# Attention and SiLU-GLU on one core: weights split into two fp32r parts at conversion, stored and reloaded as a pair

## The chip, the cores and the metric

The kernel runs on one core of a Trainium2 chip. Its engines are TensorE (PE: matmuls, with weight loads listed apart as PEld), VectorE (DVE), ScalarE (ACT), GpSimd (POOL) and SyncE (SP, which here issues every DMA). Each works through its own queue in order, and semaphores order them against each other. The metric is the time of one execution on the device in microseconds, as the median of several runs.

## The reference

Two stages, the second on the result of the first. q, k and v are float32 of shape (8, 8, 576, 64), omega is (128, 64). The three MLP weights are float64.

```python
def phi(x):                       # random features, m = 128
    proj = einsum('bhsd,md->bhsm', x, omega)
    h = proj - sum(x * x, -1) / 2
    return exp(h - max(h, -1)) / sqrt(m)
q_p, k_p = phi(q * scale), phi(k * scale)
kv = einsum('bhsm,bhsd->bhmd', k_p, v);  z = sum(k_p, axis=2)
attn = (q_p @ kv) / (q_p @ z + 1e-6)

x = attn as (4608, 512)           # tokens x model
g, val = x @ w_gate, x @ w_val    # 512 x 1536 each
out = ((g * sigmoid(g)) * val) @ w_out   # 1536 x 512
```

## The kernel before

**Attention** runs in 72 steps. Each takes two groups of 256 rows of one pair of heads: loads them (`nat`), transposes them on PE (`pt`, `st_transpose`), projects them (`pp`), takes sums of squares (`sq` on POOL) and maxima (DVE) and the exponentials (`ph` on ACT). Groups of k then add to `kvacc`. Groups of q give, through further transposes and products, columns of x, which are kept on chip as a high and a low fp32r part: ACT copies the high part (`xh`, L626) and DVE subtracts for the low part (`xl`, L627). From the step `DENSE` on, the transposes, `po` and `xt` share one PSUM bank (`ps_att`).

**The MLP** treats x as ten tiles of 512 columns (the first and last of 256), in four rounds of two or three tiles. Its hidden dimension is cut into 12 pieces f of 128, in four sets of three. A visit is one tile with one set: three gate products (`g`), the down products (`o`) of the visit before, three value products (`v`), with SiLU, the product and the split of the hidden values (`hh` on ACT, `hl` on POOL) between. Every product is made of three fp32r matmuls: high with high, and high with low both ways. Only one set of weights is on chip. Within a round the sets change three times, so that over four rounds there are 12 switches of nine weight pieces each: 108 reloads. Rounds go through the sets in alternating direction, so none is needed between rounds.

**The weights.** [...] `convert_all` turns 36 pieces of 128 x 512 float64 values into float32 (`u`) with integer and float operations on the two 32-bit halves: an absolute value on ACT (L260), five operations on DVE (L262 to L270), an add on POOL (L272). It is a generator: each `tick()` emits its next part, at a pace set by `marks`, and `need(f, i)` runs it on until piece (f, i) has been marked as converted. A raw piece is 512 KB and lies in one of two buffers (`stw`); its load is written one piece ahead. Each `u` is stored in DRAM (`wscr`, L275). The nine pieces of the first set are also split at once by `split_piece`: ACT casts to fp32r (`whi`, L242), POOL subtracts (`wlo`, L243). All others are reloaded by `load_weights` (L294) into a float32 buffer (`wraw`, three buffers, shared with `u`) and split there, as soon as PE has made its last use of the weights that they replace.

**What sets the order.** The program text is emitted step by step, with `give` mixing the MLP's work into the attention steps. Tile, the framework, then puts the instructions of each engine's queue in its own order, by when it expects them to be ready, hands out the buffers of a tag, and adds all semaphores. So a queue's order isn't that of the text: in the trace, POOL squares the input of step 66 at 811.7 us, while PE transposes it at 867.9 us.

Of the kernel before, what the change touches and what calls it, by code (L numbers as in the profile page):

```python
# [11 lines left out]
F32 = mybir.dt.float32  # L12
F32R = mybir.dt.float32r
I32 = mybir.dt.int32
U32 = mybir.dt.uint32
AF = mybir.ActivationFunctionType
ALU = mybir.AluOpType
# [6 lines left out]
def kernel(  # L24
# [11 lines left out]
    nc = tc.nc  # L36
    B, H, S, D = q.shape
    M = omega.shape[0]
    NT, DM = out.shape
    DF = w_gate.shape[1]  # L40
    P = 128
# [4 lines left out]
    NF = DF // P  # L46
# [3 lines left out]
    FA = 3  # L50
# [27 lines left out]
    wpool = ctx.enter_context(tc.tile_pool(name="wpool", bufs=FA))  # L78
    moe = ctx.enter_context(tc.tile_pool(name="moe", bufs=2))
    accp = ctx.enter_context(tc.tile_pool(name="accp", bufs=10))  # L80
    dram = ctx.enter_context(tc.tile_pool(name="dram", bufs=1, space=DRAM))
    ps_m = ctx.enter_context(tc.tile_pool(name="ps_m", bufs=4, space=PSUM))
    att = ctx.enter_context(tc.tile_pool(name="att", bufs=2))
# [36 lines left out]
    def slots(n, kind):  # L120

        if not 0 <= n < NS:
            return []
        return [(i, b, g, (kgroups if kd == "k" else qgroups)[g]) for i, (kd, b, g) in enumerate(steps[n]) if kd == kind]
# [87 lines left out]
    E_LO = float(np.uint32(896 << 20).view(np.float32))  # L212
    E_HI = float(np.uint32(1151 << 20).view(np.float32))

    wscr = dram.tile([NF, 3, P, DM], F32, name="wscr")
    raws = {}

    def load_raw(n):
        if n < 3 * NF:
            f, i = divmod(n, 3) if n >= 3 * FA else (n % FA, n // FA)  # L220
            w = (wg32, wv32, wo32)[i]
            raw = att.tile([P, 2 * DM], I32, name=f"st{f}_{i}", tag="stw")
            raws[n] = f, i, raw
            if i < 2:
                nc.sync.dma_start(
                    raw.rearrange("p (c f) -> p c f", f=2 * P),
                    w[:, f * 2 * P : (f + 1) * 2 * P].rearrange("(c p) f -> p c f", p=P),
                )
            else:
                nc.sync.dma_start(raw, w[f * P : (f + 1) * P, :])  # L230

    weights = {}
    converted = set()

    def new_weights(f, i):
        hi = wpool.tile([P, DM], F32R, name=f"whi{f}_{i}", tag=f"whi{i}")
        lo = wpool.tile([P, DM], F32R, name=f"wlo{f}_{i}", tag=f"wlo{i}")
        weights[f, i] = hi, lo

    def split_piece(f, i, raw):  # L240
        hi, lo = weights[f, i]
        nc.scalar.copy(hi, raw)  # L242
        nc.gpsimd.tensor_tensor(lo, raw, hi.bitcast(F32), op=ALU.subtract)  # L243

    OPS = 7

    def convert_all():


        load_raw(0)  # L250
        for n in range(3 * NF):
            load_raw(n + 1)
            f, i, raw = raws.pop(n)
            if f < FA:
                new_weights(f, i)
            u = moe.tile([P, DM], F32, name=f"wc{f}_{i}", tag="wraw", bufs=3)
            pairs = raw.rearrange("p (n t) -> p n t", t=2)
            low, r = pairs[:, :, 0], pairs[:, :, 1].bitcast(F32)
            ri, ui = r.bitcast(I32), u.bitcast(I32)
            nc.scalar.activation(u, r, AF.Abs)  # L260
            yield
            nc.vector.tensor_scalar(u, u, E_LO, E_HI, op0=ALU.max, op1=ALU.min)  # L262
            yield
            nc.vector.tensor_scalar(ui, ui, 3, 0x3FFFFFFF, op0=ALU.logical_shift_left, op1=ALU.bitwise_and)
            yield
            nc.vector.scalar_tensor_tensor(ri, ri, -0x40000000, ui, op0=ALU.bitwise_and, op1=ALU.bitwise_or)
            yield
            nc.vector.tensor_single_scalar(ui, ri, -0x800000, op=ALU.bitwise_and)
            yield
            nc.vector.scalar_tensor_tensor(u, low.bitcast(U32), 2.0**-52, u, op0=ALU.mult, op1=ALU.mult)  # L270
            yield
            nc.gpsimd.tensor_tensor(u, r, u, op=ALU.add)  # L272
            if f < FA:
                split_piece(f, i, u)
            nc.sync.dma_start(wscr[f, i], u)  # L275
            converted.add((f, i))
            yield

    wa = convert_all()
    ticks = [0]  # L280

# [4 lines left out]
    def need(f, i):  # L286
        while (f, i) not in converted:
            tick()

    def load_weights(f, i):  # L290
        need(f, i)
        new_weights(f, i)
        raw = moe.tile([P, DM], F32, name=f"wraw{f}_{i}", tag="wraw", bufs=3)
        nc.sync.dma_start(raw, wscr[f, i])  # L294
        split_piece(f, i, raw)

# [158 lines left out]
    def load_z(n):  # L457

        for _, b, g, gr in slots(n, "q"):
            if g == 0 and b >= BPOOL:  # L460
                assert len(converted) == 3 * NF, "the raw weights' buffers are still needed"
                zt = att.tile([P, 2, 4, M], F32, name=f"zt{b}", tag="stw")
                for a2 in range(2):
                    nc.sync.dma_start(
                        zt[:, a2], zds.pop((b, a2)).rearrange("(o h) m -> o h m", o=1).broadcast_to([P, 4, M])
                    )
                    zbc[b, a2] = zt[:, a2]
# [195 lines left out]
    def down(j, k_, ht, wts, next_set, tt):  # L663
        fs = sorted(ht)
        po = ps_moe(f"o{j}_{k_}_{tt}", [P, DM])
        for n, f in enumerate(fs):
            need(f, 2)
            mm2(po, ht[f], weights[f, 2] if wts is None else wts[f], tt, n == 0, n == FA - 1)
        if k_ == 0:
            acc[j, tt] = accp.tile([P, DM], F32, name=f"acc{j}_{tt}", tag="acc")  # L670
            nc.scalar.copy(acc[j, tt], po)
        else:
            a_ = acc[j, tt]
            nc.vector.tensor_tensor(a_, po, a_, op=ALU.add)  # L674
        if k_ == NSET - 1:
            a_ = acc.pop((j, tt))
            for o in range(0, P, RES):
                nc.sync.dma_start(rows_of(TILES[j][0] + tt * P + o), a_[o : o + RES, :])
        if next_set is not None and tt == TILES[j][1] // P - 1:
            for n in range(FA):  # L680
                load_weights(next_set * FA + n, 2)

    def stream():

        todo = []
        for vi, (j, s_, k_) in enumerate(visits):
# [22 lines left out]
            if new_set:  # L709
                for f in fs:  # L710
                    load_weights(nxt[1] * FA + f - fs[0], 0)
# [3 lines left out]
            for f in fs:  # L715
                need(f, 1)
                pv = ps_moe(f"v{vi}_{f}", [P, T])[:, 0:w]
                mm1(pv, weights[f, 1], xs)
                yield mm1_us(w)
                h = pg[f]  # L720
                nc.vector.tensor_tensor(h, pv, h, op=ALU.mult)  # L721
                hh = moe.tile([P, T], F32R, name=f"hh{vi}_{f}", tag="hh", bufs=FA)[:, 0:w]
                hl = moe.tile([P, T], F32R, name=f"hl{vi}_{f}", tag="hl", bufs=FA)[:, 0:w]
                nc.scalar.copy(hh, h)  # L724
                nc.gpsimd.tensor_tensor(hl, h, hh.bitcast(F32), op=ALU.subtract)  # L725
                ht[f] = hh, hl
                if new_set:
                    load_weights(nxt[1] * FA + f - fs[0], 1)
# [47 lines left out]
    for n in range(NN):  # L776
        load(n + LA)
        load_v(n + LAV)
        want = OPS * np.interp(clock[n + 1], [clock[m] for m, _ in marks], [x for _, x in marks])
        for i, what in enumerate(ORDER):  # L780
            left = len(ORDER) - i
            what(n)
            due = course[n + 1] - given[0] - debt[0]
            if due > 0:
                give(due / left)
            for _ in range(int(np.ceil((want - ticks[0]) / left))):
                tick()
        load_z(n)
# [32 lines left out]
```

## Time and profile before

| | |
|---|---|
| Median of 3 runs | 1264.08 us (1259.43 to 1271.75) |
| Profiled execution | 1261.98 us |
| Its span, first to last instruction | 1260.2 us |
| Mean granted clock of PE | 0.986 |
| Busy PE / PEld / DVE / ACT / POOL | 1222.5 / 1004.1 / 526.1 / 632.5 / 506.2 us |
| First raw load / last conversion add | 12.2 us / 356.3 us |
| First / last reload of a weight piece | 199.8 us / 1192.4 us |
| Last exponential of the attention | 982.6 us |

The profile is of one execution. A line names a source line (L243), an engine, an operation, and what is written and read (`wlo<-wraw,whi`); `x108` is a count. "Busy" is the time in which an engine executes; matmuls overlap in their pipeline, so their listed durations add up to more than the time they take. Waits name the engine whose signal came last. "PEclk" or the last but two of a stage's columns is the share of PE's full clock that was granted. Times to landing of a DMA run from issue to the last byte.

### The profile page before, as it was taken

How to read it: one execution, taken by the hardware profiler on the slowest of the kernel's cores; microseconds unless marked ns; L12 is line 12 of the kernel's file. 1: busy time of each engine (PE TensorE's matmuls, PEld its weight loads, DVE VectorE, ACT ScalarE, POOL GpSimd, SP SyncE). 2: the span in 40 equal slices, each digit the busy share in tenths (PEclk: the TensorE clock that was granted, in tenths of full speed). 3: DMA queues.
4: the chain of work that ended last, by engine and by line, in shares of the span. 5: the costliest groups of instructions: out<-in, count | busy, mean ns of one | idle time of the engine just before them, and what ended most of it. 6: DMA issues, size and time to landing. Idle time of an engine off the chain costs nothing.

```text
span 1260.2 us, 19027 instructions
## 1 busy us (share of the span) xinstructions
PE 1222.5 (97%) x7137; PEld 1004.1 (80%) x7137; DVE 526.1 (42%) x1080; ACT 632.5 (50%) x1368; POOL 506.2 (40%) x448
## 2 busy tenths in 40 slices
PE   6999999999899999999999999999999999999998
PEld 5888878888688878877777777877777778888887
DVE  4886795557732343334433433223343311121112
ACT  4887857564444645555556644853644323221211
POOL 3344444445442212644544334444654314242421
PEclk7999999999999999999999999999999999999999
DMA  6656555344521222222212221221211111010112
GB/s 161 152 139 154 141 146 172 106 137 122 159 67 52 61 65 60 76 67 62 65 51 67 68 59 38 64 65 45 52 50 30 39 25 50 25 51 25 51 30 55
DMA packets 157692, 97.80 MB, mean 78 GB/s; under 512 B 119680, under 2 KB 132000, under 8 KB 157600
## 3 DMA queue, kind: packets, MB, share of 16 engines
q1 hardware_dynamic: 157600, 96.59, 28.7%
q8 instruction: 56, 0.92, 0.3%
q14 instruction: 36, 0.29, 0.1%
HBM read 77.66 MB, written 18.89 MB: 77 GB/s over the span
## 4 chain that ended last, share of the span: by engine, by line
PE 67%; DVE 2%; POOL 2%; issue 1%; ACT 1%; DMA 0%; POOLq 0%; ACTq 0%
PE o L650 20%; PE g L641 19%; PE v L641 17%; PE pp L393 3%; PE kvacc L528 2%; PE ptq L552 2%; PE pt L370 2%; PE xt L607 1%; POOL jk L488 1%; PE po L569 1%; ACT ph L425 1%; DVE st L411 1%; DVE dj L492 0%; POOL wlo L243 0%; POOL hl L725 0%
## 5 line engine op out<-in xcount | busy, mean ns | idle before, releaser
L725 POOL TENSOR_TENSOR hl<-sl,hh 128x512 fp32r<-128x512 f32 (+1 forms) x120 | 145.3, 1211 | 223.0 <-ACT hh L724 222.9
L243 POOL TENSOR_TENSOR wlo<-wraw,whi 128x512 fp32r<-128x512 f32 x108 | 138.5, 1294 | 146.1 <-ACT whi L242 135.4
L425 ACT ACTIVATE ph<-pp,st 128x128 f32<-128x128 f32 x576 | 167.7, 387 | 57.7 <-DVE st L414 56.9
L641 PE MATMUL g<-xh,whi 128*128 128x512 f32 (+1 forms) x480 | 185.4, 387 | 0.0
L641 PE MATMUL v<-xh,whi 128*128 128x512 f32 (+1 forms) x480 | 184.3, 384 | 0.0
L641 PE MATMUL g<-xh,wlo 128*128 128x512 f32 (+1 forms) x480 | 179.8, 375 | 0.0
L641 PE MATMUL v<-xh,wlo 128*128 128x512 f32 (+1 forms) x480 | 179.3, 374 | 0.0
L641 PE MATMUL g<-xl,whi 128*128 128x512 f32 (+1 forms) x480 | 179.2, 373 | 0.0
L641 PE MATMUL v<-xl,whi 128*128 128x512 f32 (+1 forms) x480 | 178.5, 372 | 0.0
L650 PE MATMUL o<-whi,hh 128*128 128x512 f32 x432 | 176.5, 408 | 0.6 <-DVE sl L721 0.6
L650 PE MATMUL o<-whi,hl 128*128 128x512 f32 x432 | 169.9, 394 | 1.1 <-POOL hl L725 0.6
L650 PE MATMUL o<-wlo,hh 128*128 128x512 f32 x432 | 170.3, 394 | 0.0
L724 ACT CAST hh<-sl 128x512 fp32r<-128x512 f32 (+1 forms) x120 | 70.0, 583 | 174.5 <-DVE sl L721 174.1
L721 DVE TENSOR_TENSOR sl<-v,sl 128x512 f32<-128x512 f32 (+1 forms) x120 | 76.2, 635 | 172.2 <-PE v L641 167.9
L674 DVE TENSOR_TENSOR acc<-o,acc 128x512 f32<-128x512 f32 x108 | 74.1, 689 | 174.2 <-PE o L650 173.9
L377 POOL TENSOR_TENSOR sq<-nat 128x512 f32<-128x512 f32 x72 | 76.8, 1067 | 155.6 <-DMA nat<-in_k_dram 127.4
L411 DVE TENSOR_REDUCE st<-pp 128x4 f32<-128x512 f32 x144 | 93.5, 683 | 77.2 <-PE pp L393 77.1
L242 ACT CAST whi<-wraw 128x512 fp32r<-128x512 f32 x108 | 66.6, 622 | 97.3 <-PE v L641 55.3
L641 PEld LDWEIGHTS g<-xh,whi 128*128 128x128 f32 x480 | 91.6, 191 | 19.3 <-issue 4.2
L641 PEld LDWEIGHTS v<-xh,whi 128*128 128x128 f32 x480 | 91.0, 189 | 17.5 <-issue 2.7
L641 PEld LDWEIGHTS g<-xh,wlo 128*128 128x128 f32 x480 | 91.5, 191 | 15.9 <-issue 0.4
L641 PEld LDWEIGHTS v<-xh,wlo 128*128 128x128 f32 x480 | 91.0, 190 | 16.0 <-issue 0.5
(67 smaller groups left out, 1910.8 us busy)
## 6 DMA issues: line engine op xcount, KB each, us to landing
wraw<-wscr SPq DMA_DIRECT2D x108, 256.0 KB, 2.7
wscr<-wc SPq DMA_DIRECT2D x36, 256.0 KB, 2.3
out_dram<-acc SPq DMA_DIRECT2D x72, 128.0 KB, 2.3
nat<-in_k_dram SPq DMA_DIRECT2D x64, 128.0 KB, 3.2
v<-in_v_dram SPq DMA_DIRECT2D x64, 128.0 KB, 2.9
nat<-in_q_dram SPq DMA_DIRECT2D x64, 128.0 KB, 2.7
st<-in_moe_w_gate_dram SPq DMA_DIRECT2D x12, 512.0 KB, 4.2
st<-in_moe_w_val_dram SPq DMA_DIRECT2D x12, 512.0 KB, 4.6
```

Source lines behind the costliest of these rows:

```text
L242: nc.scalar.copy(hi, raw)
L243: nc.gpsimd.tensor_tensor(lo, raw, hi.bitcast(F32), op=ALU.subtract)
L377: nc.gpsimd.tensor_tensor(sq, nat, nat, op=ALU.mult)
L393: nc.tensor.matmul(pp[hh][:, i, c, :], x[r, i, c * P : (c + 1) * P], omT[r], start=True, stop=True)
L411: nc.vector.tensor_reduce(st[:, 1, :, :, hh], pp[hh], axis=AX.X, op=ALU.max, negate=True)
L425: nc.scalar.activation(ph[:, c, hh * M : (hh + 1) * M], pp[hh][:, i, c, :], AF.Exp, bias=st[:, 3, i, c, hh : hh + 1], scale=1.0,)
L641: nc.tensor.matmul(ps, a_[:, ws], b_[:, c, :], start=n == 0, stop=n == 3 * NC - 1)
L650: nc.tensor.matmul(ps, a_[:, ts_], b_, start=first and n == 0, stop=last and n == 2)
L674: nc.vector.tensor_tensor(a_, po, a_, op=ALU.add)
L721: nc.vector.tensor_tensor(h, pv, h, op=ALU.mult)
L724: nc.scalar.copy(hh, h)
L725: nc.gpsimd.tensor_tensor(hl, h, hh.bitcast(F32), op=ALU.subtract)
```

## The change

All 36 pieces are now split when they are converted. The nine pieces of the first set still go to their place on chip. For the other 27 the two parts, each 128 x 512 float32, are written over the raw float64 piece, which has just their size. High and low part are neighbours in one tile, so that each piece is stored by one DMA of 512 KB and reloaded by one DMA of 512 KB straight into the place from which PE reads; `split_piece` and the buffer `wraw` of the reloads are gone. A piece's store is written four DVE operations into the next piece (the last one's at the end), and only then does the piece count as converted. Raw buffers go from two to three (`zt`, which takes the same tag later, has three, too), and buffers for `u` from three to two.

```diff
-    wscr = dram.tile([NF, 3, P, DM], F32, name="wscr")
+    wscr = dram.tile([NF, 3, P, 2, DM], F32, name="wscr")
...
-            raw = att.tile([P, 2 * DM], I32, name=f"st{f}_{i}", tag="stw")
+            raw = att.tile([P, 2 * DM], I32, name=f"st{f}_{i}", tag="stw", bufs=3)
...
     def new_weights(f, i):
-        hi = wpool.tile([P, DM], F32R, name=f"whi{f}_{i}", tag=f"whi{i}")
-        lo = wpool.tile([P, DM], F32R, name=f"wlo{f}_{i}", tag=f"wlo{i}")
-        weights[f, i] = hi, lo
-
-    def split_piece(f, i, raw):
-        hi, lo = weights[f, i]
-        nc.scalar.copy(hi, raw)
-        nc.gpsimd.tensor_tensor(lo, raw, hi.bitcast(F32), op=ALU.subtract)
+        w = wpool.tile([P, 2, DM], F32R, name=f"w{f}_{i}", tag=f"w{i}")
+        weights[f, i] = w[:, 0], w[:, 1]
+        return w
...
+        def put_away(f, i, w):
+            nc.sync.dma_start(wscr[f, i], w.bitcast(F32))
+            converted.add((f, i))
+
         load_raw(0)
+        store = None
         for n in range(3 * NF):
             load_raw(n + 1)
             f, i, raw = raws.pop(n)
-            if f < FA:
-                new_weights(f, i)
-            u = moe.tile([P, DM], F32, name=f"wc{f}_{i}", tag="wraw", bufs=3)
+            u = moe.tile([P, DM], F32, name=f"wc{f}_{i}", tag="wraw", bufs=2)
...
             nc.vector.tensor_single_scalar(ui, ri, -0x800000, op=ALU.bitwise_and)
+
+            if store:
+                put_away(*store)
             yield
             nc.vector.scalar_tensor_tensor(u, low.bitcast(U32), 2.0**-52, u, op0=ALU.mult, op1=ALU.mult)
             yield
             nc.gpsimd.tensor_tensor(u, r, u, op=ALU.add)
-            if f < FA:
-                split_piece(f, i, u)
-            nc.sync.dma_start(wscr[f, i], u)
-            converted.add((f, i))
+
+            w = new_weights(f, i) if f < FA else raw.bitcast(F32R).rearrange("p (n f) -> p n f", n=2)
+            nc.scalar.copy(w[:, 0], u)
+            nc.gpsimd.tensor_tensor(w[:, 1], u, w[:, 0].bitcast(F32), op=ALU.subtract)
+            store = f, i, w
             yield
+        put_away(*store)
...
     def load_weights(f, i):
         need(f, i)
-        new_weights(f, i)
-        raw = moe.tile([P, DM], F32, name=f"wraw{f}_{i}", tag="wraw", bufs=3)
-        nc.sync.dma_start(raw, wscr[f, i])
-        split_piece(f, i, raw)
+        w = new_weights(f, i)
+        nc.sync.dma_start(w.bitcast(F32), wscr[f, i])
```

More of the change, by code (lines that the diff above doesn't have):

```diff
@@ L461, in load_z @@
                 assert len(converted) == 3 * NF, "the raw weights' buffers are still needed"
-                zt = att.tile([P, 2, 4, M], F32, name=f"zt{b}", tag="stw")
+                zt = att.tile([P, 2, 4, M], F32, name=f"zt{b}", tag="stw", bufs=3)
                 for a2 in range(2):
```

## The prediction, made before the change was run

> **What bounds the kernel now.** I read the page's busy times first, then the busy times by stage, and then what TensorE (PE) waited for.
>
> ```profile
> PE 1222.5 (97%) x7137; PEld 1004.1 (80%) x7137; DVE 526.1 (42%) x1080; ACT 632.5 (50%) x1368; POOL 506.2 (40%) x448
> ```
> ```profile
> 134.00:200.00 66.00, 62.53 (x413) 51.45 (x410) 53.99 (x116) 42.48 (x107) 26.82 (x22) 0.97 0.58 162
> 200.00:360.00 160.00, 153.40 (x853) 128.85 (x852) 95.56 (x164) 88.39 (x159) 77.64 (x62) 0.98 0.43 131
> ...
> 400.00:1050.00 650.00, 642.80 (x3593) 507.35 (x3590) 229.63 (x487) 341.00 (x703) 265.74 (x229) 1.00 0.21 54
> 1050.00:1261.00 211.00, 205.60 (x1038) 175.23 (x1036) 38.27 (x60) 51.03 (x94) 66.97 (x58) 1.00 0.16 43
> ```
> The columns are length, busy PE, PEld, DVE, ACT, POOL, clock, DMA share, GB/s. PE is the bound, and the change gives it the same matmuls. So only PE's idle time and its half clock can move: 650 - 642.80 = 7.2 us from 400 to 1050, 3.5 us from 134 to 200, 6.6 us from 200 to 360. In the conversion stage (134 to 200) DVE is busy for 53.99 of 66 us, so there a delay on DVE is nearest to PE.
>
> PE's waits, first from 400 to 1050, then from 0 to 400:
> ```profile
> PE pt L370 <- DVE xl L627: 5.7, 7, 2.0
> ```
> ```profile
> PE pt L370 <- DVE xl L627: 6.0, 1, 6.0
> ```
> One wait, seven times, makes 5.7 of the later 7.2 us: a transpose of new q and k needs the one PSUM bank that DVE's xl is still to read. What stood before xl is read from the timeline at the longest of the seven:
> ```profile
> 617.96 1.98 ACT L242 CAST whi<-wraw 128x512 fp32r<-128x512 f32 x3 [2.09 <-PE o L650]
> ...
> 620.23 3.77 POOL L243 TENSOR_TENSOR wlo<-wraw,whi 128x512 fp32r<-128x512 f32 x3
> ...
> 621.72 1.07 DVE L413 SCALAR_TENSOR_TENSOR st<-st 128x8 f32<-128x8 f32 x1
> 622.82 1.21 DVE L414 SCALAR_TENSOR_TENSOR st<-st 128x8 f32<-128x8 f32 x1
> ...
> 624.12 1.91 ACT L425 ACTIVATE ph<-pp,st 128x128 f32<-128x128 f32 x7 [4.19 <-DVE st L414]
> ...
> 627.25 0.41 DVE L627 TENSOR_TENSOR xl<-xt,xh 128x256 fp32r<-128x256 f32 x1
> ...
> 627.72 0.66 PE L370 MATMUL pt<-ident,nat 128*128 128x128 f32 x4 [2.00 <-DVE xl L627]
> ```
> ```profile
> L413 DVE SCALAR_TENSOR_TENSOR st<-st x72: 151/167/1209, 15.8 to 978.7; 128x8 f32<-128x8 f32 x72
> ```
> L413 has a median of 167 ns; it and L414 took 2.28 us together while POOL ran three weight splits: about 1.95 us too long (taking L413's median for both). The exponentials (L425) came later by that, and xl behind them. The next one:
> ```profile
> 821.24 3.78 POOL L243 TENSOR_TENSOR wlo<-wraw,whi 128x512 fp32r<-128x512 f32 x3 [8.51 <-ACT whi L242]
> ...
> 826.29 0.69 DVE L492 TENSOR_REDUCE dj<-jk 128x4 f32<-128x512 f32 x1 [4.96 <-POOL jk L488]
> ...
> 827.96 0.66 PE L370 MATMUL pt<-ident,nat 128*128 128x128 f32 x4 [1.20 <-DVE xl L627]
> ```
> Here jk stood behind three splits on POOL, and DVE, with xl queued, behind jk.
>
> **What is removed.** Each of 108 reloads loses one ACT cast and one POOL subtract:
> ```profile
> L243 POOL TENSOR_TENSOR wlo<-wraw,whi x108: 1268/1291/1492, 206.8 to 1203.6; 128x512 fp32r<-128x512 f32 x108
> ```
> ```profile
> L242 ACT CAST whi<-wraw x108: 605/621/643, 205.6 to 1201.7; 128x512 fp32r<-128x512 f32 x108
> ```
> By stage (length, then busy POOL in those instructions alone):
> ```profile
> 134.00:200.00 66.00, 1.34 (x1) 0.97 0.58 162
> 200.00:360.00 160.00, 27.45 (x21) 0.98 0.43 131
> 360.00:1261.00 901.00, 111.00 (x87) 1.00 0.20 52
> ```
> After 360 us POOL loses 111 us and ACT 87 x 0.621 = 54 us. PE gets only what waited for them, the two stalls above: 2.0 + 1.2 = 3.2 us. To that comes the clock:
> ```profile
> 625.00:630.00 5.00, 3.00 (x13) 2.16 (x12) 1.72 (x4) 2.67 (x9) 3.57 (x3) 0.83 0.24 67
> 630.00:635.00 5.00, 5.00 (x27) 4.28 (x25) 1.41 (x3) 0.81 (x2) 2.29 (x2) 0.83 0.24 53
> ...
> 340.00:344.00 4.00, 0.83 (x5) 0.84 (x5) 3.64 (x6) 3.15 (x9) 2.85 (x3) 0.69 0.58 178
> 344.00:348.00 4.00, 4.00 (x12) 3.13 (x11) 0.00 (x0) 1.72 (x5) 2.12 (x2) 0.50 0.64 176
> ```
> The first stall was followed by 10 us at 0.83: 1.7 us more. Term one: -4.9 us (bounds: -8.9, all 7.2 us of idle time and the clock; +2, one such stall new, since the order on each engine is planned afresh).
>
> The Trainium skill ("TensorE: Matmul & The Clock Gate", HAM oscillation) asks for an idle window of about 3.4 us before the clock halves. The trace differs: an idle time of 2.0 us was followed by the low clock, and the sum goes by the trace; by the page's rule the result would be 1.7 us higher.
>
> **What is added.** The 27 later pieces (36 less the 9 that were already split at conversion) now get that cast and subtract as they are converted. The conversion's own POOL add shows their pace:
> ```profile
> L272 POOL TENSOR_TENSOR wc<-st,wc x36: 1290/1306/1494, 21.1 to 356.3; 128x512 f32<-128x512 f32 x36
> ```
> Ten of those adds start from 134 to 200 us and 17 from 200 to 360 (counted in the rows of that group). So from 134 to 200 POOL gains 10 x 1.291 = 12.9 us and ACT 6.2 us, with nothing taken out; from 200 to 360 the balance is 17 in, 21 out. In the first stretch the cost lies between two rates: 87 splits after 360 us cost PE 4.9 us, 0.06 each, so 0.6 us; and the stall at 627 us cost 2.0 per three, so 6.7 us. I take 2, nearer the low end, since L413's median shows that most instructions meet no split. Term two: +2 us.
>
> **The conversion's buffers.** Near 340 us PE stood for 6.0 us and then ran at 0.69 and 0.50: 4 x 0.31 + 4 x 0.50 = 3.2 us more, 9.2 in all. ACT had waited for a float64 piece just before:
> ```profile
> 330.17 1.31 POOL L272 TENSOR_TENSOR wc<-st,wc 128x512 f32<-128x512 f32 x1 [2.85 <-DVE wc L270]
> ...
> 335.98 0.67 ACT L260 ACTIVATE wc<-st 128x512 f32<-128x512 f32 x1 [3.27 <-DMA st<-in_moe_w_val_dram]
> ...
> 342.31 1.30 POOL L272 TENSOR_TENSOR wc<-st,wc 128x512 f32<-128x512 f32 x1 [1.15 <-DVE wc L270]
> ```
> ```profile
> wraw<-wscr SPq DMA_DIRECT2D x108, 256.0 KB, 2.7
> wscr<-wc SPq DMA_DIRECT2D x36, 256.0 KB, 2.3
> ...
> st<-in_moe_w_out_dram SPq DMA_DIRECT2D x12, 512.0 KB, 3.9
> ```
> A raw buffer now is free for the next load after the add of its piece: from the add at 330.17 to that of the piece that took the buffer, at 342.31, are 12.1 us, for two buffers 6.1 us a piece. With three, each is also held through cast and subtract (0.62 + 1.29) and a store of 512 KB (3.9, as w_out's load): 12.1 + 5.8 = 17.9, or 6.0 a piece. The rush before the third switch stays as tight as it was, and its stall may fall elsewhere or return. That a piece counts as converted only at its store, four DVE operations into the next piece, lets the MLP's calls pull that much conversion forward; the time is in the same bounds. u's buffers go from three to two, but each is free after add, cast and subtract, 3.2 us, below those 6. Term three: -2 us (bounds -9.2 and +9.2, the stall gone or doubled).
>
> **The reload.** A set's weights now leave DRAM only when PE has read the old ones, where before they waited on chip, unsplit.
> ```profile
> 211.30 0.40 PE L641 MATMUL g<-xh,wlo 128*128 128x512 f32 x1
> ...
> 221.50 0.36 PE L641 MATMUL g<-xh,whi 128*128 128x256 f32 x1
> ```
> ```profile
> 1110.91 4.31 PE g L641 x36
> ...
> 1127.72 8.19 PE g L641 x36
> ```
> 512 KB in rows of 4 KB took 3.9 us (w_out's load), 11.7 us if three ran wholly one after another. At the first switch the last of the three old gate weights is read at 211.7 us, the first new one at 221.5: 9.8 us, and the other two loads leave before, as their own readers end. In the last round the gate's readers end at 1115.2 and start at 1127.7, 12.5 us on. I cost it at nothing: the down and value matmuls between cover it. Without that cover it would be 3.9 us at each of 36 groups. The stores grow to 512 KB, 2.3 to about 3.9 us, and nobody waits for them but raw loads (above).
>
> **SP's queue** held its reloads behind POOL, and its stores behind the add:
> ```profile
> SPq L294 <- POOL wlo L243: 386.5, 87, 40.0
> ...
> SPq L275 <- POOL wc L272: 122.2, 29, 12.8
> ```
> The second goes, the store being issued a piece later; the first becomes a wait for PE. Behind it stand raw loads, q, k and v. The splits themselves waited for PE, so the moment hardly moves: zero.
>
> **Sum.** The profiled execution took 1262.0 us (span 1260.2), 2.1 below the median of 1264.1. 1262.0 - 4.9 + 2 - 2 = 1257.1, so 1257.
>
> **Rivals.**
> *Faster:* everything held by ACT's and POOL's waits comes earlier from 134 us on. All idle time from 134 to 360 (10.1), its low clock (0.03 x 66 + 0.02 x 160 = 5.2), and 8.9 later are 24 us; three quarters give 1244. For: whi waits in ACT's queue for PE, as at 617.96. Against: from 134 to 200 work is added.
> *Nothing:* the splits were off the path, and a new order trades stalls: 1262. For: 3.2 us of stalls against 111 us of POOL.
> *Slower, the SP queue:* in the first round a reload waits on SP for PE's last read, and a raw load stands behind it; ACT, in order, then waits at L260 as at 335.98, and hh, the exponentials and xh with it. If each of the round's three switches makes a stall like the one near 340 us, two are new: 1262 - 4.9 + 2 + 2 x 9.2 = 1278. It decides once raw loads leave over 4 us later than the piece before is done. Against: SP waited before, too.
> *Slower, the port:* each of the ten splits from 134 to 200 us stops DVE for its whole 1.29 us, as L413's longest, 1.209, allows: 1262 - 4.9 + 12.9 = 1270. Against: L413's median. The Trainium skill ("SBUF — State Buffer", Who interferes with whom) states such an exclusive lock between GpSimd and DVE instructions with two SBUF inputs; L413's maximum agrees.
>
> **Chances.** Forecast 0.43, faster 0.23, nothing 0.14, SP queue 0.13, port 0.07. About 1% (12.6 us: 1251.4 to 1276.7) is what a measurement here can tell from no change. Faster by more: most of the second case and the forecast's lower tail (all of term one's and three's bounds), 0.27. Slower by more: most of the SP case and a little of the port's, 0.15. Within: 0.58. The range runs from the faster case to just past the port's, 1243 to 1273; it leaves out the SP case and the faster one's tail.
>
> **What would show it.** Right: L294 with no L242 or L243 beside it and 512 KB in about 4 us; POOL near 506 - 104 = 402 us and ACT near 632 - 50 = 582; L413's long cases rarer after 400 us; pt's wait for xl from 400 to 1050 down from 5.7 to 2 or 3; PE never waiting for a weight load. Wrong: PE waiting for w; ACT's waits at L260 for raw loads longer, with a low clock after them; more idle PE from 134 to 200.

## The result and the profile after

The changed kernel takes 1267.76 us (median of 20 runs, 1264.06 to 1278.86), the kernel before 1260.32 (20 runs beside them, 1257.32 to 1271.83). The ratio is 1.0062, 95% interval 1.0041 to 1.0083: slower by 0.6%, where 0.4% faster was forecast.

The profiled execution of after is the longest of its 20 (1278.86 us, span 1277.1), so it is read here for waits, counts and places, and not for the total. The busy line of its page, and the same stretches as before (length, busy PE, PEld, DVE, ACT, POOL with their instructions, clock, DMA share, GB/s):

```profile
PE 1236.0 (97%) x7137; PEld 1018.2 (80%) x7137; DVE 522.2 (41%) x1080; ACT 589.5 (46%) x1291; POOL 404.7 (32%) x367
```
```profile
134.00:200.00 66.00, 60.30 (x368) 51.20 (x366) 48.44 (x103) 44.29 (x102) 33.24 (x27) 0.85 0.58 165
200.00:360.00 160.00, 148.05 (x831) 124.33 (x831) 102.00 (x183) 85.55 (x169) 78.05 (x62) 0.98 0.63 202
400.00:1050.00 650.00, 644.42 (x3605) 509.51 (x3604) 228.24 (x491) 314.80 (x652) 198.03 (x176) 1.00 0.28 78
```
The first 134 us, before and then after:

```profile
0.00:134.00 134.00, 118.21 (x1018) 106.76 (x1019) 96.65 (x233) 95.45 (x279) 54.47 (x65) 0.92 0.59 145
```
```profile
0.00:134.00 134.00, 121.07 (x983) 110.29 (x983) 91.21 (x219) 90.58 (x266) 49.69 (x62) 0.87 0.57 153
```
The engines did what the diff says: POOL fell by 101.5 us, ACT by 43.0. From 400 to 1050 us PE won 1.6 us of busy time. From 134 to 200 us it got 368 instructions done where before had 413, at a clock of 0.85 against 0.97, and from 200 to 360 us 831 against 853. The 35 instructions fewer ahead of 134 us, where none of the 27 pieces has been split yet, went with a longer time at half clock, and e1 below, which has the change but for the place of a store, has none of that: 1034 up to 134 us, then 392 and 823. In both the loss lies in the conversion. These counts are the measure in what follows, one execution each: PE's whole work is the same 7137 instructions in every kernel here.

PE's waits (us in total, times, longest) from 134 to 360 us in before, in after and in e8, which is after with the subtract on VectorE and runs 10 us faster; in the next fence those of after from 400 to 1050:

```profile
PE po L569 <- DVE xl L627: 2.8, 5, 1.6
```
```profile
PE po L571 <- DVE xl L629: 11.1, 4, 6.3
```
```profile
PE po L571 <- DVE xl L629: 9.4, 3, 6.5
```
```profile
PE pt L372 <- DVE xl L629: 2.1, 4, 1.1
PE pt L372 <- issue: 1.9, 1, 1.9
```
DVE's xl, on which 5.7 us hung after 400 us, holds PE there for 2.1 us now; but one new gap of 1.9 us has come. Before 360 us the same xl holds PE for 11.1 us, where in before it held po for 2.8 and pt for 6.0. The timeline of after shows what stood before the longest of these, 6.3 us (L415 and L416 are before's L413 and L414):

```profile
294.50 1.48 POOL L274 TENSOR_TENSOR wc<-st,wc 128x512 f32<-128x512 f32 x1 [3.35 <-DVE st L415]
294.74 1.25 DVE L416 SCALAR_TENSOR_TENSOR st<-st 128x8 f32<-128x8 f32 x1
296.08 1.28 ACT L427 ACT_TABLE_LOAD   x1 [5.58 <-DVE st L416]
...
298.17 0.42 DVE L629 TENSOR_TENSOR xl<-xt,xh 128x256 fp32r<-128x256 f32 x1
...
298.64 0.69 PE L571 MATMUL po<-kvr,qt 128*128 128x65 f32 x2 [6.32 <-DVE xl L629]
```
L416 took 1.25 us beside the conversion's own add, the pattern of 621 us in before. But that explains some 1.1 of the 6.3 us: VectorE also had the operations of two pieces to convert, from 289.6 us on, ahead of xl. And the stall is not what the split costs: in e8 the same matmul, the 209th of the 320 of po, waits 6.5 us with L416 at 0.16 us, and e8 is no slower than before. Of the 144 instructions of these two lines, 7 took over 0.5 us after 400 us in before and 1 in after; from 200 to 360 us it is 1 and 5.

The lines of the reload and of its queue in after:

```profile
w<-wscr SPq DMA_DIRECT2D x108, 512.0 KB, 4.2
wscr<-st SPq DMA_DIRECT2D x27, 512.0 KB, 3.2
```
```profile
SPq L297 <- PE g L643: 186.7, 33, 37.3
...
SPq L225 <- DMA wscr<-st: 16.6, 10, 2.3
SPq L230 <- DMA wscr<-st: 13.4, 8, 2.4
```
The reload now waits for PE's last reading, as its diff implies, and no matmul or weight load of PE waits for w anywhere in the trace.

### The profile page after: what moved, and what is told of

Same layout as the page of the kernel before. It is cut to its first block, busy times and chain, and to the rows that moved or that the text cites. A ratio compares the mean times of both kernels' runs of the same rounds, so it can differ in the third digit from the quotient of the medians.

```text
span 1277.1 us, 18735 instructions
## 1 busy us (share of the span) xinstructions
PE 1236.0 (97%) x7137; PEld 1018.2 (80%) x7137; DVE 522.2 (41%) x1080; ACT 589.5 (46%) x1291; POOL 404.7 (32%) x367
## 4 chain that ended last, share of the span: by engine, by line
PE 85%; DVE 5%; POOL 3%; ACT 3%; DMA 2%; issue 2%; SPq 1%; ACTq 0%; POOLq 0%; DVEq 0%
PE o L652 22%; PE g L643 22%; PE v L643 20%; PE pp L395 6%; PE kvacc L530 5%; PE pt L372 3%; PE po L571 2%; PE ptq L554 2%; PE xt L609 1%; ACT ph L427 1%; POOL wc L274 1%; DMA st<-in_moe_w_gate_dram 1%; DVE st L413 1%; POOL hl L727 1%; SPq L330 1%
## 5 line engine op out<-in xcount | busy, mean ns | idle before, releaser
L643 PE MATMUL g<-xh,w 128*128 128x512 f32 (+1 forms) x960 | 296.6, 379 | 0.0
L643 PE MATMUL v<-xh,w 128*128 128x512 f32 (+1 forms) x960 | 295.5, 379 | 0.0
L652 PE MATMUL o<-w,hh 128*128 128x512 f32 x864 | 281.5, 405 | 3.0 <-DVE sl L723 1.7
L643 PEld LDWEIGHTS g<-xh,w 128*128 128x128 f32 x960 | 175.5, 189 | 34.8 <-issue 4.6
L643 PEld LDWEIGHTS v<-xh,w 128*128 128x128 f32 x960 | 175.7, 190 | 33.6 <-issue 3.2
L652 PEld LDWEIGHTS o<-w,hh 128*128 128x128 f32 x864 | 157.4, 190 | 37.6 <-issue 5.5
L643 PE MATMUL v<-xl,w 128*128 128x512 f32 (+1 forms) x480 | 178.9, 373 | 0.0
L643 PE MATMUL g<-xl,w 128*128 128x512 f32 (+1 forms) x480 | 178.6, 372 | 0.0
L652 PE MATMUL o<-w,hl 128*128 128x512 f32 x432 | 171.3, 397 | 3.7 <-POOL hl L727 3.2
L413 DVE TENSOR_REDUCE st<-pp 128x4 f32<-128x512 f32 x144 | 93.4, 683 | 88.9 <-PE pp L395 88.6
L395 PE MATMUL pp<-omT,x 64*128 64x128 f32 x1152 | 100.9, 304 | 2.0 <-ACT x L380 1.1
L643 PEld LDWEIGHTS v<-xl,w 128*128 128x128 f32 x480 | 91.3, 190 | 13.7 <-issue 0.4
```

The costliest lines, as they stand in the source:

```text
L395: nc.tensor.matmul(pp[hh][:, i, c, :], x[r, i, c * P : (c + 1) * P], omT[r], start=True, stop=True)
L413: nc.vector.tensor_reduce(st[:, 1, :, :, hh], pp[hh], axis=AX.X, op=ALU.max, negate=True)
L643: nc.tensor.matmul(ps, a_[:, ws], b_[:, c, :], start=n == 0, stop=n == 3 * NC - 1)
L652: nc.tensor.matmul(ps, a_[:, ts_], b_, start=first and n == 0, stop=last and n == 2)
```

## The experiments

The theory after the first look: the split of a piece as it is converted costs more than the reload gains. Rivals: the reload itself, the third raw buffer with its longer holds, the store's place, ScalarE's or GpSimd's queue standing, GpSimd's computing. In the expectations, theory S is that the moved splits cost PE, theory B that the late store and the third raw buffer let conversions crowd ahead of the attention's work on VectorE. All ratios are to the kernel before, measured beside the run.

### The two halves of the change

The split left out, first as after has the rest, then with two raw buffers and the store at once:

```diff
-            w = new_weights(f, i) if f < FA else raw.bitcast(F32R)...
-            nc.scalar.copy(w[:, 0], u)
-            nc.gpsimd.tensor_tensor(w[:, 1], u, w[:, 0].bitcast(F32), op=ALU.subtract)
+            if f < FA:    (as before)
+            else:
+                w = u.rearrange("p (o f) -> p o f", o=1).broadcast_to([P, 2, DM])
```


> The changed kernel without the cast and the subtract of the 27 later pieces at conversion: both halves of the stored pair are the unsplit weight, so the products with those weights are not the reference's; stores and reloads keep their sizes, u has three buffers. Theory S: faster than before, 0.993 to 0.998. Theory B: still slower, 1.003 to 1.007.

> As e5_raw2, but without the cast and the subtract of the 27 later pieces at conversion: both halves of the stored pair are the unsplit weight, so the products with those weights are not the reference's; u has three buffers. It is the reload's half of the change alone, on the kernel before's conversion. Theories B and S both: 0.994 to 0.999. If it stays above 1.002, the reload itself (512 KB straight into place) costs time.

Measured: 1.0031 (1.0015 to 1.0047) for the first, 0.9944 (0.9925 to 0.9964) for the second. The direct reload by itself gains 0.56%, about 7 us. The first came out as theory B had it: with three raw buffers and the late store the kernel is slower than before even without the split, and leaving the split out wins only 0.31% (1.0062 to 1.0031), about 4 us. The kernel before with a split added that nobody reads, and the kernel of the second run with the split put back:

```diff
+            else:
+                w = raw.bitcast(F32R).rearrange("p (n f) -> p n f", n=2)
+                nc.scalar.copy(w[:, 0], u)
+                nc.gpsimd.tensor_tensor(w[:, 1], u, w[:, 0].bitcast(F32), op=ALU.subtract)
```


> The kernel before, with the cast and the subtract of the 27 later pieces done at conversion as well, into the raw buffer, where nobody reads them; stores, reloads and the splits at the reload as before. Theory S: 1.005 to 1.010. Theory B: 0.999 to 1.003.

> The changed kernel with the store straight behind the split and only two raw buffers. If the third buffer is what lets conversions crowd together (theory B), 1.000 to 1.003; if the moved splits are the cost (theory S), a raw piece is now also held through split and store, and it is no faster than with three: 1.004 to 1.008.

Measured: 1.0109 (1.0088 to 1.0130) and 1.0102 (1.0064 to 1.0140). (The diff is that of the first of the two.) The split at conversion costs 1.1% on the kernel before and 1.6% (0.9944 to 1.0102) with the direct reload and two raw buffers. In after's own arrangement it was 0.3%. So the reload is not the cause and the split is one; its price depends on the buffers and the order around it, and the prices do not add up.

### Buffers and the store's place

The kernel before with three raw buffers and nothing else, and after with each store straight behind its split:

```diff
-            raw = att.tile([P, 2 * DM], I32, name=f"st{f}_{i}", tag="stw")
+            raw = att.tile([P, 2 * DM], I32, name=f"st{f}_{i}", tag="stw", bufs=3)
```


> The kernel before, with three raw buffers in place of two and nothing else. Theory S: no change, 0.998 to 1.002. Theory B: slower, 1.003 to 1.007, with conversions earlier and stalls of pt or po for xl between 200 and 360 us.

> The changed kernel, with each piece's store written straight behind its own split, not four DVE operations into the next piece. Theory S (the 27 splits that moved into the conversion stage cost PE there): about as the changed kernel, ratio 1.005 to 1.008. Theory B (bunching: the late store and the third raw buffer let conversions crowd in front of the attention's DVE work): 1.000 to 1.003, and the 6.3 us stall near 292 us gone.

Measured: 1.0049 (1.0027 to 1.0071; 12 runs from 1258.04 to 1271.99) and 1.0051 (1.0037 to 1.0064). Three raw buffers cost the kernel before 0.5%, where I had the stall near 340 us go or return. With the split in, three look better than two (e1 against e5, 1.0051 to 1.0102, intervals that touch); without it two are better by 11 us (e3 against e6, 1.0031 to 0.9944, where the store's place differs too). Why they cost without it is not settled: e2's profiled execution was one of its short ones (1258.9 us) and has as many PE instructions from 134 to 200 us as before, 413. The store's place changes nothing that can be told (after 1.0062, e1 1.0051, intervals overlapping).

### Which of the split's two instructions

After with the subtract of the 27 later pieces on VectorE:

```diff
-            nc.gpsimd.tensor_tensor(w[:, 1], u, w[:, 0].bitcast(F32), op=ALU.subtract)
+            (nc.gpsimd if f < FA else nc.vector).tensor_tensor(w[:, 1], u, ...
```


> The changed kernel with the subtract of the 27 later pieces on DVE (0.69 us each) in place of POOL (1.29 us each). If POOL's subtracts cost by stopping DVE's instructions, faster than the changed kernel: 1.001 to 1.004. If DVE's queue ahead of xl is what counts, slower: 1.008 to 1.015.

Measured: 0.9985 (0.9962 to 1.0009), 10 us less than after, though VectorE is the busier engine in that stage. The same edit in the kernel of e5, with two raw buffers:

> The kernel of e5 (after, each store straight behind its split, two raw buffers as before the change; ratio 1.010) with the subtract of the 27 later pieces on VectorE in place of GpSimd. If the price of the split in e5 is that GpSimd's queue stands in the split, most of the 20 us between e5 and e6 goes: 0.994 to 0.999, about 1254 us. If the price is that the raw buffer is held through the split and the store, whoever computes it, the run stays near e5: 1.005 to 1.011.

Measured: 0.9990 (0.9969 to 1.0011), against e5's 1.0102. The raw buffer is held through cast, subtract and store in both, so that the hold is not the price either. Then the two instructions one at a time, dead, on the kernel before:

```diff
+                nc.scalar.copy(w[:, 0], u)                                  (e9)
+                nc.gpsimd.tensor_tensor(w[:, 1], u, u, op=ALU.subtract)     (e10)
```


> The kernel before, with one dead cast added for each of the 27 later pieces: ScalarE copies the converted piece, right behind GpSimd's add, into the upper half of the spent raw buffer, and nothing reads it. No subtract is added; the reload is as before. It takes the first half of the split of e4 alone (e4: ratio 1.011 with cast and subtract). If the price of the split is ScalarE's queue standing still behind a cast that waits for GpSimd's add (the trace after has 45.1 us of such waits between 134 and 360 us), this run has that wait whole and should keep most of it: 1.005 to 1.011, about 1270 us where before is 1260. If the price is GpSimd's time or its own wait for the cast, this run has neither and should be 0.998 to 1.003.

> The kernel before, with one dead subtract added for each of the 27 later pieces: GpSimd subtracts the converted piece from itself, right behind its own add, into the spent raw buffer, and nothing reads it; ScalarE gets nothing. It is the second half of the split of e4 without the hop over ScalarE. If GpSimd's added time (27 instructions of some 1.3 us) is the price, the run should be 1.006 to 1.011, about 1270 us. If the price is the hop (ScalarE waits for the add, GpSimd for the cast), the subtract finds its operands ready and the run should be 0.998 to 1.003, since 35 us of work on an engine that is idle most of the time is hidden.

Measured: cast 1.0012 (0.9992 to 1.0031), subtract 1.0077 (1.0057 to 1.0097). ScalarE's queue stood behind its cast for nearly as long as in after (first line: e9, second: after; both from 134 to 360 us), and no cost can be told:

```profile
ACT st L277 <- POOL wc L272: 37.9, 21, 5.0
```
```profile
ACT st L277 <- POOL wc L274: 45.1, 18, 5.3
```
I had taken those 45.1 us, and the ping-pong between the two queues, for the cause. The counter-test, cast and subtract both on GpSimd so that no queue waits for the other within a split:

```diff
-            nc.scalar.copy(w[:, 0], u)
+            if f < FA:
+                nc.scalar.copy(w[:, 0], u)
+            else:
+                nc.gpsimd.tensor_copy(w[:, 0], u)
```


> The kernel after, with the cast of the 27 later pieces on GpSimd in place of ScalarE, so that add, cast and subtract follow one another on one engine and no queue waits for another within a split. GpSimd gains 27 casts, ScalarE loses them. If the hop between the queues is the price, the run should win most of what the subtract on VectorE won (e8: 10 us less than after): 0.997 to 1.002, about 1260 us where after is 1268. If GpSimd's time is the price, it should be no better than after: 1.006 to 1.015.

Measured: 1.0129 (1.0107 to 1.0151). Without the hop it is worse than after. The price goes with what GpSimd computes.

### By which path

In the trace of e10 the attention's squares stand behind the dead subtract (L277) on GpSimd, VectorE's queue stands at their reduction, and xl behind it:

```profile
177.32 1.11 POOL L277 TENSOR_TENSOR st<-wc 128x512 fp32r<-128x512 f32 x1
178.39 1.04 POOL L380 TENSOR_TENSOR sq<-nat 128x512 f32<-128x512 f32 x1
...
179.46 0.69 DVE L407 TENSOR_REDUCE st<-sq 128x8 f32<-128x512 f32 x1 [1.93 <-POOL sq L380]
...
182.86 1.10 PE L572 MATMUL po<-kvr,qt 128*128 128x65 f32 x8 [2.57 <-DVE xl L630]
```
In before the same two waits are 0.93 and 1.58 us: the squares' delay is PE's delay there. Twelve steps' squares moved to VectorE, in after, in before, and in e10:

```diff
-        nc.gpsimd.tensor_tensor(sq, nat, nat, op=ALU.mult)
+        if not 24 <= n < 36:
+            nc.gpsimd.tensor_tensor(sq, nat, nat, op=ALU.mult)
...
+            nc.vector.tensor_tensor(sq, nat, nat, op=ALU.mult)    (ahead of the reduction)
```


> The kernel after, with the squares of the attention's steps 24 to 35 on VectorE, directly ahead of the reduction that reads them, in place of GpSimd, where they stand behind the split's subtract. First theory: GpSimd's time per piece costs by one path, the squares come late, VectorE's queue stands at the reduction with the subtract xl behind it, and TensorE waits for xl. Then the squares leave that path and the run should be about 9 us better than after: 0.995 to 1.001 of before. Rival: GpSimd's time costs by another path (the next piece's add, the hidden layer's low part, or VectorE held by GpSimd), and the run stays at 1.003 to 1.009.

> The kernel before, with the same twelve squares on VectorE: the control for the next run, and for the one ahead of this. VectorE gains some 8 us of work, GpSimd loses 13.5 us, spread over 200 us. Both theories: 0.996 to 1.005.

> The kernel before with the dead subtract of each of the 27 later pieces on GpSimd, as in e10 (ratio 1.0077), and with the twelve squares on VectorE, as in the control of this call. First theory (the split's time on GpSimd costs by the squares that stand behind it): no more than 0.003 above the control. Rival (another path): 0.006 to 0.010 above the control, as e10 stands to the kernel before.

Measured: 1.0048 (1.0035 to 1.0061), 0.9987 (0.9967 to 1.0008) and 1.0070 (1.0054 to 1.0085). The dead subtract costs 0.8% over its control as it did with the squares in place: the price does not need that path. The two traces run the same order on every engine but for the added subtracts (and so do those of before and e10, but for two DMA issues). The largest single difference between them is shown by the timeline (start, duration in us) of e14, the control:

```profile
166.74 0.68 DVE L409 TENSOR_TENSOR sq<-nat 128x512 f32<-128x512 f32 x1
...
167.34 0.68 DVE L266 SCALAR_TENSOR_TENSOR st<-st,wc 128x512 int32<-128x512 int32 x1
...
172.25 1.11 PE L576 MATMUL po<-kvr,qt 128*128 128x65 f32 x8 [1.19 <-DVE xl L634]
```
and of e15, with the dead subtract (L277):

```profile
169.10 1.47 POOL L272 TENSOR_TENSOR wc<-st,wc 128x512 f32<-128x512 f32 x1
169.35 1.78 DVE L412 TENSOR_TENSOR sq<-nat 128x512 f32<-128x512 f32 x1
...
170.65 1.37 POOL L277 TENSOR_TENSOR st<-wc 128x512 fp32r<-128x512 f32 x1
...
171.05 1.52 DVE L266 SCALAR_TENSOR_TENSOR st<-st,wc 128x512 int32<-128x512 int32 x1
...
176.77 1.54 PE L579 MATMUL po<-kvr,qt 128*128 128x65 f32 x6 [2.90 <-DVE xl L637]
```
Each of two VectorE instructions ends 0.5 to 0.6 us after the GpSimd instruction that it overlaps, 1.78 and 1.52 us instead of 0.68: 1.94 us more ahead of xl, and PE waits 2.90 us where it had waited 1.19. The first of the two is held by the conversion's own add, which e14 has too: the subtract also shifts what meets what. Instruction by instruction, VectorE's work of 134 to 200 us took 2.6 us longer in e15 than in e14, and 0.6 us longer in e10 than in before. Is it this, or still GpSimd's queue? One kernel holds the queue and computes next to nothing, the other computes as long as e10 but reads nothing:

```diff
+                nc.scalar.copy(w[:, 0], u)                                               (e16)
+                nc.gpsimd.tensor_tensor(w[:, 1, 0:8], u[:, 0:8], w[:, 0, 0:8]..., op=ALU.subtract)
...
+                nc.gpsimd.memset(raw.bitcast(F32), 0.0)                                  (e17)
```


> The kernel before, and for each of the 27 later pieces a dead cast on ScalarE, then a dead subtract of only eight columns on GpSimd that reads the cast. GpSimd's queue stands behind the add for as long as in e4 (it waits for the cast) but computes nothing in that time, and the 128x512 subtract is gone. If the price of the split is that what stands behind it on GpSimd comes later (a held queue), this run keeps it: 1.006 to 1.011. If the price is that VectorE's instructions stand still while GpSimd computes on tiles in SBUF, the run is near e9, which has the cast alone: 0.998 to 1.003.

> The kernel before, with a dead memset of the whole spent raw buffer (128x1024) on GpSimd for each of the 27 later pieces, in the place of e10's dead subtract: by the row of v's memset (128x520 in 531 ns) 1.05 us each, as long as e10's subtract (1.09 us), but it reads nothing. If any time on GpSimd costs, 1.006 to 1.010, as e10. If only reads of GpSimd hold VectorE, 0.998 to 1.002. By the Trainium skill (SBUF — State Buffer, section Who interferes with whom) VectorE's instructions with two inputs in SBUF contend only with a GpSimd instruction that reads, the one-input forms in a two-port mode with any. By that rule about half of the price stays, 1.002 to 1.006.

Measured: 1.0010 (0.9994 to 1.0026) and 1.0076 (1.0045 to 1.0106). The groups on GpSimd from 134 to 360 us (busy us, mean ns, then idle before), e16, then e10, then e17:

```profile
L278 POOL TENSOR_TENSOR st<-wc,st 128x8 fp32r<-128x8 f32 x26 | 6.3, 240 | 18.8 <-ACT st L277 18.0 <-DMA st<-in_moe_w_val_dram 0.7
```
```profile
L277 POOL TENSOR_TENSOR st<-wc 128x512 fp32r<-128x512 f32 x26 | 28.4, 1091 | 2.0
```
```profile
L276 POOL MEMSET st<- 128x1024 f32 x26 | 26.1, 1004 | 1.4
```
In e16 GpSimd's queue is taken for 6.3 + 18.8 = 25.1 us, of which it computes 6.3: no cost that can be told. In e17 it computes 26.1 us: the whole cost of e10. So it is GpSimd's computing during the conversion that slows the kernel. That a held queue is free is shown less surely: e9 and e16 also run another order (some 240 of PE's 7137 instructions stand elsewhere than in before; in e17, 14), and in e10 work that stood behind the subtract did hold PE, as shown. The memset holds VectorE too, seen in e17's timeline:

```profile
334.95 1.11 POOL L276 MEMSET st<- 128x1024 f32 x1
335.20 1.14 DVE L264 TENSOR_SCALAR wc<-wc 128x512 int32<-128x512 int32 x1
...
341.04 0.43 DVE L264 TENSOR_SCALAR wc<-wc 128x512 int32<-128x512 int32 x1
...
347.54 1.19 POOL L276 MEMSET st<- 128x1024 f32 x1
347.93 0.69 DVE L266 SCALAR_TENSOR_TENSOR st<-st,wc 128x512 int32<-128x512 int32 x1
```
L264 (one input) ends 0.28 us after the memset, 1.14 us where it takes 0.43 alone; L266 (two inputs) runs through a memset in its usual 0.69, but took 1.52 beside a subtract. The Trainium skill ("SBUF — State Buffer", Who interferes with whom) has that distinction: two inputs contend only with GpSimd's reads, a one-input form in a two-port mode with either. The rows agree. By that rule I had estimated about half of the subtract's price for the memset; it cost all of it, so the measurement decides for the kernel's time, and how the price parts between the forms stays open.

### Where in time

After with only the first ten of the 27 subtracts on VectorE:

```diff
+            (nc.vector if 9 <= n < 19 else nc.gpsimd).tensor_tensor(w[:, 1], u, ...
```


> The kernel after, with the subtract of only the first ten of the 27 later pieces (those converted between about 134 and 200 us) on VectorE; the other 17 stay on GpSimd. With all 27 on VectorE (e8) the ratio was 0.9985, with none (after) 1.0062. If the loss sits between 134 and 200 us, where the change adds splits and takes none away, this run is as good as e8: 0.996 to 1.001. If each of the 27 splits costs alike, ten of them give back 10/27 of the 0.0077 between e8 and after: about 1.003, 1.002 to 1.006.

Measured: 1.0016 (0.9992 to 1.0041), between the two expectations and not apart from either: ten of the 27 give back 0.0046 of 0.0077, by its interval from a quarter to nine tenths. Its stretches, then e10's, then the first one of e3, which has no split of these pieces:

```profile
134.00:200.00 66.00, 62.06 (x427) 51.88 (x427) 55.33 (x123) 47.17 (x116) 27.34 (x23) 0.97 0.64 183
200.00:360.00 160.00, 149.64 (x809) 124.50 (x807) 103.50 (x178) 81.46 (x161) 74.13 (x59) 0.96 0.60 196
```
```profile
134.00:200.00 66.00, 59.15 (x346) 48.81 (x345) 47.88 (x99) 36.92 (x91) 32.92 (x28) 0.87 0.47 137
200.00:360.00 160.00, 151.04 (x860) 126.92 (x859) 99.19 (x170) 87.94 (x166) 92.43 (x77) 0.98 0.44 136
```
```profile
134.00:200.00 66.00, 59.04 (x368) 49.36 (x367) 53.10 (x109) 37.99 (x93) 27.38 (x22) 0.87 0.68 196
```
With GpSimd back at 27.34 us from 134 to 200 us PE does 427 instructions there (before 413, after 368). From 200 to 360 us it stays at 809 (before 853). In e10 all of the loss is in the first stretch. So with before's order the first stretch answers to GpSimd's time. In after's arrangement that is not the whole of it: e3 has GpSimd at 27.38 us there, as e18, and only 368 instructions of PE, as after. Why it has, and why after loses 22 instructions, and e18 44, in the second stretch, where GpSimd has no more to do than before, one profiled execution of each does not tell, and it stays open.

### A version that beats both

The split at a piece's first reload in place of the conversion: conversion as before, the pair stored from there, the other 81 reloads direct. It computes the full result.

```diff
     def load_weights(f, i):
         need(f, i)
-        new_weights(f, i)
+        w = new_weights(f, i)
+        if (f, i) in put:
+            nc.sync.dma_start(w.bitcast(F32), wsp[f, i])
+            return
         raw = moe.tile([P, DM], F32, name=f"wraw{f}_{i}", tag="wraw", bufs=3)
         nc.sync.dma_start(raw, wscr[f, i])
-        split_piece(f, i, raw)
+        split_piece(f, i, raw, w)      (and stores the pair to wsp)
```


> Conversion as in the kernel before (u stored, two raw buffers). A later piece is split when it is first reloaded, as before, and its two parts are then stored as a pair from the place where PE reads them; the other 81 reloads are direct. If the conversion stage is what the change pays for and the direct reload what it gains by: 0.994 to 0.999. If neither reload nor conversion but any new order costs: 1.002 or more.

Measured: 0.9967 (0.9948 to 0.9986), 1256.69 us. From 134 to 360 us its GpSimd has the work that it had before:

```profile
134.00:200.00 66.00, 60.51 (x414) 50.12 (x414) 50.79 (x117) 42.17 (x106) 26.49 (x22) 0.97 0.64 180
200.00:360.00 160.00, 153.22 (x842) 129.21 (x843) 94.55 (x162) 86.90 (x156) 77.57 (x61) 0.98 0.60 197
```

## Why the prediction was wrong, step by step

**Bound and place: right.** PE's work stayed the same and only its gaps and its clock moved; the stretch that I named as the nearest to PE, 134 to 200 us, is where PE lost most in the profiled executions of after and e10 (in e1 it lost 21 instructions there and 30 from 200 to 360).

**Term one, -4.9 us: right in kind.** POOL's 404.7 us and ACT's 589.5 stand against 402 and 582 foretold. Both stalls that the term rested on are gone, and pt's wait for xl fell to 2.1 us, within the 2 to 3 foretold; L413's long cases did become rare after 400 us. A new gap of 1.9 us came in the profiled execution, the "new stall" of its bound. All that the direct reload gains, with the splits before 360 us, measures 7 us (e6).

**Term two, +2 us: this is the step that failed.** Mis-sized. I took the rate between 0.06 us a split (seen after 400 us, where VectorE is busy 35% of the time) and 0.67, chose near the lower end because L413's median meets no split, and called the 17 in and 21 out after 200 us even. Measured, the 27 subtracts alone cost 9.7 us (e10, 0.77% of 1260; e8 wins as much back in after), the whole split 13.7 (e4), on the direct reload with two buffers some 20 (e5 against e6), and only about 4 in after's own arrangement (against e3). By e10 that is 0.36 us for each of the 27, where the term's 2 us make 0.07. Two things were wrong in the working. L413 was a weak row to take the rate from: in before, from 134 to 360 us, L413 and L414 ran over 0.15 us above their lower quartiles in 2 of 24 cases, the conversion's own five VectorE instructions, 0.4 to 0.7 us on whole tiles, in 38 of 132. And the term had no low clock in it, though term one had put 1.7 us of it to a stall of 2.0; two thirds of e10's loss from 134 to 200 us is clock (below).

**Term three, -2 us: wrong in sign, inside its bounds of 9.2 on the kernel before.** The third raw buffer costs that kernel 0.5%, some 6 us (e2); without the split, on the direct reload and with the late store, 11 (e3 against e6). With the split it does not cost (e1 against e5). The sum took its terms as independent, and the runs show that they are not.

**Reload and SP's queue, zero: right.** 512 KB landed in 4.2 us for an estimated 3.9, PE waited for no weight, and raw loads waited for a store's landing in 30.0 us of SP's time (16.6 and 13.4), with no stall of PE behind it that I could find. The rival by SP's queue, at 1278, fell.

**The port rival, 1270 at a chance of 0.07: nearest of all to the 1267.8 measured, and the one to which I gave the least.** It named the right engine; that its number came so near is luck. Its price had each of the ten splits hold DVE for its whole length, 12.9 us, where the holds of that stretch grew by 0.6 us (e10) and 2.6 (e15). What the runs show is that GpSimd's computing costs (e10, e17, e8), and in e15 two VectorE instructions held for 0.84 and 1.10 us, ahead of a longer wait of PE. What they don't show is a sum: over all of 134 to 360 us VectorE's instructions are no longer in after than before by the traces' durations (27.8 and 27.7 us too long: each instruction's duration less its line's lower quartile, summed where that is over 0.15 us), and in e10, where no split has left the reload, they are 29.7. So it would be the holds' place that decides, not their total; that is read from e15, where late squares are out of the way, and not isolated.

**The clock makes much of it.** From 134 to 200 us PE of e10 stood idle for 6.85 us, of before for 3.47: 3.4 us more. Its clock was 0.87 against 0.97: 0.10 x 66 = 6.6 us more, in kernels of the same order. For e15 against e14, from 134 to 360 us, it is 4.2 us of idle time (15.9 against 11.8) and some 5 of clock (0.95 and 0.97 against 1.00 and 0.98 in the two stretches). Two stretches of after, at its longest half-clock period behind 134 us:

```profile
180.00:184.00 4.00, 2.05 (x18) 1.86 (x19) 4.00 (x7) 3.33 (x10) 3.43 (x3) 0.90 0.59 192
184.00:200.00 16.00, 16.00 (x66) 14.06 (x65) 8.37 (x21) 6.39 (x17) 6.09 (x6) 0.50 0.36 108
```
Within these 4 us PE was idle for 1.95, and 16 us at 0.50 followed: 8 us lost to 2 of waiting. I had put 1.7 us on a stall of 2.0.

## What to carry to other kernels

Work moved to an engine that is half idle is not free if its stage also has the engine that feeds the bound one (VectorE here, busy for 54 of 66 us): 27 subtracts on GpSimd cost 9.7 us. Take the rate from instructions of the stage it moves to, with whole tiles, and not from a median elsewhere, and add the low clock that follows a stall. When a change has two halves, measure each on the old kernel; here one gained 7 us and the other lost twice that on the old kernel, though not in every arrangement, and keeping the first (e7) beat both kernels. A long wait in a table of waits is no cause by itself: 37.9 us of them were added in e9 at no cost that can be told, and a stall of 6.5 us stood in e8, which is no slower than before.

## What the runs showed of the hardware

A memset of GpSimd, which reads nothing, costs the kernel as much as a subtract of nearly the same length (1.0076 and 1.0077; 1.00 and 1.09 us each). A GpSimd queue taken for 25.1 us, 18.8 of them standing still, costs nothing that can be told (1.0010), in a kernel whose order changed too. And stalls of about 2 us in PE are followed by half-clock periods of very different length: the one after the stall of 2.0 us near 628 us in before cost 1.7 us, the one after 1.95 us of idle time at 180 to 184 us in after cost 8.
